# Two token tiles by plain products at the head of pass one, and x's split operands kept in DRAM for pass two

## The chip, the cores and the metric

The kernel runs on one core of a Trainium2 chip. The metric is the device time of one execution in microseconds (us). The engines are PE (TensorE, the matrix unit; PEld is its weight load), DVE (VectorE), ACT (ScalarE), POOL (GpSimd) and SP (SyncE, which issues all DMAs of this kernel).

## The reference

Chunked attention (chunks of 64 tokens) is followed by two feed-forward blocks over 4608 tokens, all in float32:

```python
attn = softmax(0.125 * q_c @ k_c.T) ; x = attn @ v_c     # 8x8 heads of 64, as 4608 x 512
h = x @ w_in          # 512 -> 2048
g = h * np.cos(h)
x2 = g @ w_out        # 2048 -> 512
a = x2 @ w1 ; b = x2 @ w2     # 512 -> 1024 each
out = ((a * b) @ w3) @ w_out2 # 1024 -> 1024 -> 512
```

## The kernel before

**Float32 on PE.** Each operand is split into two parts, a high one rounded for PE and the low rest (`split`: ACT writes the high part, DVE or POOL subtracts to get the low one). A product is then three matmuls (`mm3`: high x high, high x low, low x high; lines 97 to 99).

**Tiles and groups.** The tokens are cut into 9 tiles of 512. The 2048 columns of `w_in` are cut into 8 groups of 256. Pass one takes all nine tiles through groups 0 to 4 and stores its part of x2 (`x2a`); pass two takes them through groups 5 to 7, starting with tile 8 and going on with 0 to 7, and adds (`L529`). Then comes the second block, `ab_mm` and `out_mm`. One round of the loop over `i` is one group of one tile: the products of x with `w_in` (42 matmuls of 256 columns), the chain h*cos(h) on ACT and DVE, and the product of the group before with `w_out` (`x2_mm`, 24 matmuls of 512 columns, in halves `x` and `y`).

**Seven products.** `Seven` computes the 2x2 block product of x and `w_in` with seven block products in place of eight. For this it needs seven operands of x (B11, B21, T2, T1, T3, B22, T4; the T are sums made by `x_sums` and line 408, each of the seven is split by `x_op`) and, of each pair of weight blocks, sums too (lines 175 to 178, split into W pieces 2 and 3). Partial results are combined by DVE out of PSUM into tiles `d` and `e` (lines 440, 450, 452, 459); by this the PSUM bank comes free. `bank_h` has two banks.

**Weights.** A weight arrives as int64 words and is converted by `conv_tick` in a pipeline: load, `conv_a` (ACT line 115, DVE lines 116 and 117), `conv_b` (POOL line 123), `conv_c` (ACT high part, POOL or DVE low part, line 205). Twenty weights (`cq`) are converted in the head and in tile 0. All others are staged through DRAM in pass one and two (`st_load` to `st_lo`, then `pump` loads them, `w<-sd`).

**The order of the work** is written by hand: `START` for the attention of tile 0, and one string of letters per kind of group. In them digits are the steps of `Seven`; `q` is one of five steps of attention for the next tile (scores, exp, scale on POOL, transposes, values); `a A b B` and `c C d D` are the cosine chains of `d` and `e` (`a` ACT, `A` DVE, `b` ACT, `B` DVE); `s` splits g; `w`, `v` are conversions; `l m h r` stage one weight; `S T o` make and split the operands of the next tile's x. In pass one x lies in `xf` and is also stored to `xd` (line 368); in pass two `xf` is loaded from `xd` (line 738) and the seven operands are made again in the last group of each tile (`ORDER3E`).

Of the kernel before, what the change touches and what calls it, by code (L numbers as in the profile page):

```python
# [51 lines left out]
def chunk_attention_two_ffn(  # L52
# [108 lines left out]
    def conv_c(key, lo_eng):  # L161

        pair, second = pair_of(key)
        m = halfway.pop(key).bitcast(F32)
        if not second:
            t = new_w(key if pair is None else (pair, 0))
            nc.scalar.activation(t[:, 0], m, AF.Copy)
            if pair:
                firsts[pair] = m
            return [(lo_eng, t, m)]  # L170
        a = firsts.pop(pair)
        a11, a12, a21, a22 = a[:, 0:256], a[:, 256:512], m[:, 0:256], m[:, 256:512]
        s23 = spare[:, 0]
        s2, s3, s4 = s23[:, 0:256], s23[:, 256:512], spare[:, 1, 0:256]
        nc.vector.tensor_tensor(out=s3, in0=a11, in1=a21, op=ALU.subtract)
        nc.vector.tensor_tensor(out=a21, in0=a21, in1=a22, op=ALU.add)
        nc.vector.tensor_tensor(out=s2, in0=a21, in1=a11, op=ALU.subtract)
        nc.vector.tensor_tensor(out=s4, in0=a12, in1=s2, op=ALU.subtract)
        t, ts = new_w((pair, 1)), new_w((pair, 2))
        t4 = new_s4((pair, 3))  # L180
        for d, x in ((t, m), (ts, s23), (t4, s4)):
            nc.scalar.activation(d[:, 0], x, AF.Copy)
        return [(nc.vector, t, m), (nc.vector, ts, s23), (nc.gpsimd, t4, s4)]
# [4 lines left out]
    def conv_tick(lo_eng=None):  # L188

        last = []  # L190
        if cat[3] < cat[2]:
            key = cq[cat[3]]
            pair, second = pair_of(key)
            if not free(slots, 1 + second) or second and not free(s4s, 1):
                return False
            last = conv_c(key, lo_eng or nc.gpsimd)
            cat[3] += 1
# [155 lines left out]
    def att_values(j, early):  # L353
# [467 lines left out]
```

## Time and profile before

| | us |
|---|---|
| three runs | 1597.18, 1601.99, 1604.14 |
| median | 1601.99 |
| profiled execution, its own time | 1598.41 |
| span of the profile | 1596.6 |
| PE busy | 1503.7 (94%) |
| DVE busy | 1187.9 (74%) |
| ACT busy | 799.2 (50%) |
| POOL busy | 344.8 (22%) |

The profiled execution took 1.8 us more than its span. PE is busy nearly everywhere except at the head and in a stretch of pass two, so a stretch is read by what PE does in it and what it waits for. The boundaries used below are the starts of groups on PE: the first product with `w_in` is at 45.49, tile 1 begins at 145.31, tile 2 at 214.50, tile 3 at 279.10, pass two at 655.9.

### The profile page before, as it was taken

What the parts mean: (1) busy time and instruction counts of PE and PEld (TensorE: products, weight loads), DVE (VectorE), ACT (ScalarE), POOL (GpSimd) and SP (SyncE); (2) the same over time, 40 slices, a digit from 0 to 9 for tenths busy, and PEclk for the clock granted to TensorE, in tenths of its full rate; (3) what the DMA queues carried; (4) which work ended last, traced back from release to release, by engine and by line L of the source; (5) the groups of instructions that cost most, each with busy time, mean ns of one, the idle gap of its engine ahead of it and who ended that gap; (6) DMA issues with size and microseconds to landing.
All of it is one profiled execution on the core that took longest, in us unless ns stands there. A gap on an engine that the chain in (4) does not pass through costs nothing.

```text
span 1596.6 us, 28424 instructions
## 1 busy us (share of the span) xinstructions
PE 1503.7 (94%) x11280; PEld 1358.8 (85%) x11280; DVE 1187.9 (74%) x1868; ACT 799.2 (50%) x1366; POOL 344.8 (22%) x257
## 2 busy tenths in 40 slices
PE   4578999999999999989999999899999999999998
PEld 3467888888888888978888888799999999999997
DVE  7997888887887877788888888736656556566564
ACT  3666887877878776555555555312212212122121
POOL 3766222222322222222222122110000000000000
PEclk8689999999999999999999999999999999999999
DMA  6432445445435435956555454951011011010000
GB/s 207 136 119 73 166 149 175 146 139 167 164 127 166 136 110 201 370 183 220 207 194 196 178 194 171 388 198 53 1 54 53 1 53 54 1 53 30 25 27 27
DMA packets 86100, 212.09 MB, mean 133 GB/s; under 512 B 9552, under 2 KB 12368, under 8 KB 82768
## 3 DMA queue, kind: packets, MB, share of 16 engines
q1 hardware_dynamic: 85968, 210.28, 37.9%
q8 instruction: 89, 1.46, 0.4%
q14 instruction: 43, 0.35, 0.1%
HBM read 133.43 MB, written 76.81 MB: 132 GB/s over the span
## 4 chain that ended last, share of the span: by engine, by line
PE 71%; DVE 14%; DMA 7%; ACT 5%; issue 2%; SPq 1%; DVEq 0%; ACTq 0%
PE acc L97 9%; PE acc L98 9%; PE acc L99 9%; PE ps_hh L97 9%; PE ps_hh L99 8%; PE ps_hh L98 8%; PE ps_aa L97 4%; PE ps_aa L98 4%; PE ps_aa L99 4%; DMA w<-sd 2%; PE ps_at L362 2%; PE ps_s L322 2%; DVE x2a L529 1%; DMA xf<-xd 1%; ACT T L92 1%
## 5 line engine op out<-in xcount | busy, mean ns | idle before, releaser
L500 POOL TENSOR_TENSOR g<-t,g 128x512 fp32r<-128x512 f32 x144 | 203.2, 1432 | 593.0 <-ACT g L499 410.2
L97 PE MATMUL acc<-g,w 128*128 128x512 f32 x576 | 231.1, 401 | 0.0
L92 ACT ACTIVATE phl<-e 128x512 fp32r<-128x512 f32 x72 | 45.5, 632 | 363.6 <-DVE e L598 355.5
L98 PE MATMUL acc<-g,w 128*128 128x512 f32 x576 | 226.9, 394 | 0.1
L99 PE MATMUL acc<-g,w 128*128 128x512 f32 x576 | 226.0, 392 | 0.0
L97 PE MATMUL ps_hh<-T,w 128*128 128x256 f32 x720 | 208.8, 290 | 6.7 <-ACT x L432 6.6
L98 PE MATMUL ps_hh<-T,w 128*128 128x256 f32 x720 | 205.9, 286 | 0.3 <-POOL T L93 0.3
L99 PE MATMUL ps_hh<-T,w 128*128 128x256 f32 x720 | 205.7, 286 | 0.0
L440 DVE TENSOR_TENSOR d<-x,ps_hh 128x512 f32<-128x512 f32 x144 | 98.5, 684 | 136.1 <-PE ps_hh L99 112.7
L97 PE MATMUL ps_hh<-B,w 128*128 128x256 f32 x576 | 167.0, 290 | 1.2 <-ACT B L92 1.2
L98 PE MATMUL ps_hh<-B,w 128*128 128x256 f32 x576 | 163.9, 285 | 3.0 <-DVE B L93 3.0
L99 PE MATMUL ps_hh<-B,w 128*128 128x256 f32 x576 | 163.6, 284 | 0.0
L97 PEld LDWEIGHTS ps_hh<-T,w 128*128 128x128 f32 x720 | 139.9, 194 | 10.1 <-ACT x L432 7.6
L98 PEld LDWEIGHTS ps_hh<-T,w 128*128 128x128 f32 x720 | 139.9, 194 | 1.4 <-POOL T L93 0.7
L99 PEld LDWEIGHTS ps_hh<-T,w 128*128 128x128 f32 x720 | 140.1, 195 | 0.0
L476 ACT ACTIVATE t<-d 128x512 int32<-128x512 f32 x72 | 45.5, 632 | 170.3 <-DVE d L452 168.1
L99 PEld LDWEIGHTS acc<-g,w 128*128 128x128 f32 x576 | 109.3, 190 | 23.9
L98 PEld LDWEIGHTS acc<-g,w 128*128 128x128 f32 x576 | 110.3, 192 | 20.3 <-POOL g L500 0.6
L97 PEld LDWEIGHTS acc<-g,w 128*128 128x128 f32 x576 | 110.3, 191 | 19.8
L98 PE MATMUL ps_aa<-T,w 128*128 128x256 f32 x432 | 122.4, 283 | 0.4 <-DVE T L93 0.4
L97 PE MATMUL ps_aa<-T,w 128*128 128x256 f32 x432 | 122.3, 283 | 0.0
L99 PE MATMUL ps_aa<-T,w 128*128 128x256 f32 x432 | 122.2, 283 | 0.0
(138 smaller groups left out, 3891.3 us busy)
## 6 DMA issues: line engine op xcount, KB each, us to landing
w<-sd SPq DMA_DIRECT2D x63, 512.0 KB, 8.0
sd<-raw SPq DMA_DIRECT2D x104, 256.0 KB, 2.3
qk<-in_q_dram SPq DMA_DIRECT2D x36, 256.0 KB, 3.9
qk<-in_k_dram SPq DMA_DIRECT2D x36, 256.0 KB, 4.1
vt<-in_v_dram SPq DMA_DIRECT2D x36, 256.0 KB, 3.0
x2a<-x2o SPq DMA_DIRECT2D x36, 256.0 KB, 2.6
x2a<-x2a SPq DMA_DIRECT2D x36, 256.0 KB, 7.6
x2d<-x2a SPq DMA_DIRECT2D x36, 256.0 KB, 4.8
```

The source lines that it names most:

```text
L92: nc.scalar.activation(dst[:, 0], src, AF.Copy)
L97: nc.tensor.matmul(ps, a[0], b[0], start=first, stop=False)
L98: nc.tensor.matmul(ps, a[0], b[1], start=False, stop=False)
L99: nc.tensor.matmul(ps, a[1], b[0], start=False, stop=last)
L322: nc.tensor.matmul(s3[r, h], qk[r, 0, h], qk[r, 1, h], start=True, stop=True)
L362: nc.tensor.matmul(o[r, h, t], vt[r, c, h], pt[r, h, t], start=True, stop=True)
L440: nc.vector.tensor_tensor(out=two(self.d), in0=self.x1.unsqueeze(1).to_broadcast([P, 2, 256]), in1=two(p26), op=ALU.add)
L476: nc.scalar.activation(t.bitcast(I32), h, AF.Copy, scale=INV2PI)
L500: nc.gpsimd.tensor_tensor(out=lo, in0=r, in1=f32(hi), op=ALU.subtract)
L529: nc.vector.tensor_tensor(out=t, in0=t, in1=acc[c], op=ALU.add)
```

## The change

**Tiles 0 and 1 by plain products.** For the first ten groups `Plain` replaces `Seven`: eight block products (48 matmuls of 256 columns) straight into two banks, one bank holding what `d` held, the other `e`. No sums of x or of weights are needed, and x has four operands in place of seven. The cosine chain reads the PSUM banks themselves.

**Weights.** In the conversion `conv_b` and every low part move from POOL to DVE; the sums of weight pairs are no longer made there. The converted `w_in` is also stored to DRAM (`wr`), and loaded again in tiles 1 and 2 (`L`), where the sums are made and split (`M`, `H`, `R`), one group per round.

**x in DRAM.** For tiles 2 to 7 the seven split operands are stored in pass one (7 x 512 KB, `xs`) in place of x (1 MB, `xd`). In pass two they are loaded straight into the operands' tiles, each after the last product that reads it (`load_x`), and the last group of such a tile (`ORDER3X`) makes no sums and no splits. Staging takes the eight `wo2` first. All splits of x are on DVE, where `LO` had put some on POOL for the first group strings.

```diff
-ORDER0 = "1sw2qq5qa3cAewbCBxqdyvDqw"
-ORDER1 = "1s2qh5qqa3clAexqbCrmBdyqD"
+ORDER0 = "PsvqQqacvAqCxvqbBdyvDq"
+ORDER0E = "PsvQacvACxobBodyDoo"
+ORDER1P = "PsqMhQqqHaclAxqbCrRmBdyqDL"
+ORDER1PE = "SPsQacATCoobBoxodoDyoo"
+ORDER1 = "1s2qMh5qqHa3clAxqbCrRmBdyqDL"
 ORDER3E = "S1sT25a3cACoobBoxodoDyoo"
+ORDER3X = "1s25a3cACbBxdDy"
...
-        nc.gpsimd.tensor_tensor(out=m, in0=m, in1=raws.pop(key)[:, :, 0].bitcast(I32), op=ALU.add)
+        nc.vector.tensor_tensor(out=m, in0=m, in1=raws.pop(key)[:, :, 0].bitcast(I32), op=ALU.add)
+        if key[0] == "in":
+            nc.sync.dma_start(out=wr[key[1] // 2][:, key[1] % 2], in_=m.bitcast(F32))
...
+    def sum_load(g):
+        pair = ("in", g)
+        sp["at"] = pair, new_w((pair, 2))
+        nc.sync.dma_start(out=f32(W[pair, 2]), in_=wr[g])
+
+    def sum_make():
...
+        nc.vector.tensor_tensor(out=s3, in0=a11, in1=a21, op=ALU.subtract)
+        nc.vector.tensor_tensor(out=s1, in0=a21, in1=a22, op=ALU.add)
+        nc.vector.tensor_tensor(out=s2, in0=s1, in1=a11, op=ALU.subtract)
+        nc.vector.tensor_tensor(out=s4, in0=a12, in1=s2, op=ALU.subtract)
...
+    def sum_lo():
+        for d, x in sp.pop("parts"):
+            nc.vector.tensor_tensor(out=d[:, 1], in0=x, in1=f32(d[:, 0]), op=ALU.subtract)
...
+    def x_op(op, keep=None):
 
         d = X[op].rearrange("p s (c t) -> p s c t", c=2)
-        split(d, xv[op], nc.vector if los[-1][OPS.index(op)] == "v" else nc.gpsimd)
+        split(d, xv[op], nc.vector)
+        if keep in xs:
+            nc.sync.dma_start(out=xs[keep][op], in_=f32(X[op]))
...
+    class Plain:
...
+        def half(self, blocks):
+            p = bank_h()
+            for n, (e, ops) in enumerate(blocks):
+                w, ps = self.w[e], p[:, 256 * n:256 * n + 256]
+                for c in range(4):
+                    m, x, t = slice(P * c, P * c + P), X[ops[c // 2]], slice(256 * (c % 2), 256 * (c % 2) + 256)
+                    mm3(ps, (w[:, 0, m], w[:, 1, m]), (x[:, 0, t], x[:, 1, t]), c == 0, c == 3)
+            return p
+
+        def stepP(self):
+            self.d = self.half([(0, ("B11", "B21")), (1, ("T1", "B22"))])
+
+        def stepQ(self):
+            self.e = self.half([(0, ("T1", "B22")), (1, ("B11", "B21"))])
...
-            return ORDER3E if end else ORDER3B if nth else ORDER3
+            return (ORDER3X if k_tile in xs else ORDER3E) if end else ORDER3B if nth else ORDER3
...
+            def load_x(op):
+                nc.sync.dma_start(out=f32(X[op]), in_=xs[k_tile][op])
+
+            z = Plain(("in", g)) if i < 2 * GA else Seven(
+                ("in", g), (bank_h,) * 4, False, load_x if ps and end and k_tile in xs else None)
...
-                if nth == 0:
+                if nth == 0 and k_tile not in xs:
                     nc.sync.dma_start(out=xf, in_=xd[k_tile] if k_tile + 1 < NTILE else x2d[order[0]])
```

DVE in the second group of tile 0 before: the cosine chain (L481, L491) with conversions and the sums of a weight pair (L175 to L178) between its steps.

```order
L481 SCALAR_TENSOR_TENSOR t<-d,t 128x512
L116 TENSOR_SCALAR cw<-raw 128x512
L117 SCALAR_TENSOR_TENSOR cw<-raw,cw 128x512
L481 SCALAR_TENSOR_TENSOR t<-e,t 128x512
L491 TENSOR_TENSOR t<-t,d 128x512
L175 TENSOR_TENSOR spare<-cw 128x256
L176 TENSOR_TENSOR cw<-cw 128x256
L177 TENSOR_TENSOR spare<-cw 128x256
L178 TENSOR_TENSOR spare<-cw,spare 128x256
```

The same place in the changed kernel: the chain is L529 and L539 there and reads the bank `ps_hh`, the conversion is L128, L121, L122, L195.

```order
L529 SCALAR_TENSOR_TENSOR t<-ps_hh,t 128x512
L358 TENSOR_REDUCE sm<-ex 128x8
L359 TENSOR_SCALAR sm<-sm 128x8
L361 RECIPROCAL rc<-sm 128x8
L529 SCALAR_TENSOR_TENSOR t<-ps_hh,t 128x512
L128 ISA cw<-raw,cw 128x1024
L121 TENSOR_SCALAR cw<-raw 128x512
L122 SCALAR_TENSOR_TENSOR cw<-raw,cw 128x512
L195 TENSOR_TENSOR w<-cw,w 128x512
L539 TENSOR_TENSOR t<-t,ps_hh 128x512
```

The weight sums are gone from here, and a conversion (one POOL instruction of it now on DVE, as L128) stands between the chain's two halves.

DVE in pass two before, from the last group of a tile into the first of the next: the splits of x (L93) and one sum (L408) stand among the chain's steps and ahead of L440, which frees a bank.

```order
L481 SCALAR_TENSOR_TENSOR t<-e,t 128x512
L93 TENSOR_TENSOR B_119<-xf,B_119 128x512
L93 TENSOR_TENSOR B_120<-xf,B_120 128x512
L491 TENSOR_TENSOR t<-t,d 128x512
L93 TENSOR_TENSOR T_121<-spare,T_121 128x512
L408 TENSOR_TENSOR xf<-xf,spare 128x2x256
L93 TENSOR_TENSOR T_122<-spare,T_122 128x512
L93 TENSOR_TENSOR T_123<-xf,T_123 128x512
L491 TENSOR_TENSOR t<-t,e 128x512
L93 TENSOR_TENSOR B_124<-xf,B_124 128x512
L93 TENSOR_TENSOR T_125<-xf,T_125 128x512
L440 TENSOR_TENSOR d<-x_9088,ps_hh 128x512
```

The same place in the changed kernel (L529 and L539 are the chain, L466 is what L440 was):

```order
L529 SCALAR_TENSOR_TENSOR t<-e,t 128x512
L539 TENSOR_TENSOR t<-t,d 128x512
L539 TENSOR_TENSOR t<-t,e 128x512
L466 TENSOR_TENSOR d<-x_9112,ps_hh 128x512
L291 TENSOR_TENSOR raw<-cw,raw 128x512
```

Eight instructions ahead of L440 are gone (three sums more stood earlier in the group).

SP at that place in the changed kernel: the seven loads (L733) stand between the loads of x2 (L588) and the first store of the next staged weight (L294).

```order
L588 DMA x2a<-x2a_133 128x512 x4
L733 DMA B_166<-xs3B_96 128x1024
L733 DMA B_167<-xs3B_97 128x1024
L733 DMA T_168<-xs3T_98 128x1024
L733 DMA T_169<-xs3T_99 128x1024
L733 DMA T_170<-xs3T_100 128x1024
L733 DMA B_171<-xs3B_101 128x1024
L733 DMA T_172<-xs3T_102 128x1024
L294 DMA sd_9144<-raw 128x512
```

Before, L540 (the loads of x2) is followed there by the store L273 at once; the load of `xf` stood one group earlier.

## Rows read from the trace of the kernel before

**Rows 1.** Windows: us; PE, PEld, DVE, ACT, POOL busy; PEclk; DMA share; GB/s.

```profile
0.00:45.49 45.49, 19.43 (x272) 16.88 (x273) 35.12 (x57) 19.59 (x35) 17.73 (x19) 0.83 0.59 199
45.49:145.31 99.82, 71.18 (x578) 61.81 (x579) 89.78 (x106) 60.47 (x100) 69.66 (x48) 0.80 0.37 124
145.31:214.50 69.19, 66.15 (x603) 58.65 (x602) 58.07 (x94) 52.65 (x85) 23.02 (x18) 0.98 0.40 134
214.50:279.10 64.60, 64.60 (x604) 57.14 (x602) 55.63 (x96) 52.26 (x85) 17.83 (x14) 1.00 0.48 160
764.70:1005.60 240.90, 227.42 (x1333) 201.96 (x1332) 207.08 (x325) 136.91 (x247) 53.79 (x36) 0.99 0.55 190
```

**Rows 2.** Timeline of the head: start, duration, engine, line, operation, idle time before.

```profile
26.65 0.42 DVE L116 TENSOR_SCALAR cw<-raw 128x512 uint32<-128x512 uint32 x1
27.10 0.69 DVE L117 SCALAR_TENSOR_TENSOR cw<-raw,cw 128x512 uint32<-128x512 uint32 x1
27.71 0.69 DVE L205 TENSOR_TENSOR w<-cw,w 128x512 fp32r<-128x512 f32 x1
27.93 1.60 POOL L123 TENSOR_TENSOR cw<-cw,raw 128x512 int32<-128x512 int32 x1 [3.07 <-ACT raw L115]
28.43 1.39 DVE L116 TENSOR_SCALAR cw<-raw 128x512 uint32<-128x512 uint32 x1
...
29.85 1.65 DVE L117 SCALAR_TENSOR_TENSOR cw<-raw,cw 128x512 uint32<-128x512 uint32 x1
```

**Rows 3.** Groups by line and form: busy us, mean ns of one; idle before.

```profile
L242 DVE CUSTOM_DVE_ANT_0 cw<-raw,cw 128x1024 uint16<-128x1024 uint16 x52 | 36.0, 693 | 7.0 <-DVE cw L240 0.5
...
L326 DVE TENSOR_TENSOR ex<-ps_s,mx 128x512 f32<-128x512 f32 x36 | 24.9, 692 | 2.7
...
L337 DVE TENSOR_REDUCE sm<-ex 128x8 f32<-128x512 f32 x36 | 24.4, 678 | 0.9 <-ACT ex L332 0.9
```

**Rows 4.** The same view: POOL's part of g's split, and its scale.

```profile
L500 POOL TENSOR_TENSOR g<-t,g 128x512 fp32r<-128x512 f32 x144 | 203.2, 1432 | 593.0 <-ACT g L499 410.2 <-DVE B L93 143.6 <-PE ps_hh L99 39.2
...
L341 POOL TENSOR_TENSOR ex<-ex,rc 128x512 f32<-128x512 f32 x32 | 33.5, 1045 | 72.2 <-DVE rc L340 72.2
```

**Rows 5.** Timeline of DVE in tile 0's fourth group, where no conversion is left.

```profile
132.60 0.69 DVE L491 TENSOR_TENSOR t<-t,d 128x512 f32<-128x512 f32 x1 [2.13 <-ACT t L487]
...
134.35 0.69 DVE L491 TENSOR_TENSOR t<-t,e 128x512 f32<-128x512 f32 x1 [1.06 <-ACT t L487]
```

**Rows 6.** Timeline of PE: matmuls of 256 columns, first at half clock, then full.

```profile
70.89 0.41 PE L97 MATMUL ps_hh<-B,w 128*128 128x256 f32 x1
71.11 0.41 PE L98 MATMUL ps_hh<-B,w 128*128 128x256 f32 x1
...
71.47 0.28 PE L97 MATMUL ps_hh<-T,w 128*128 128x256 f32 x1
71.59 0.28 PE L98 MATMUL ps_hh<-T,w 128*128 128x256 f32 x1
```

**Rows 7.** Windows over three groups of pass two; columns as in Rows 1.

```profile
764.70:775.20 10.50, 10.50 (x67) 9.54 (x66) 7.45 (x13) 6.49 (x12) 2.55 (x2) 1.00 0.48 187
775.20:788.50 13.30, 13.30 (x80) 11.83 (x79) 12.40 (x20) 6.32 (x13) 3.15 (x2) 1.00 0.35 120
788.50:806.40 17.90, 15.00 (x80) 13.12 (x79) 15.83 (x28) 10.99 (x20) 2.50 (x2) 0.90 0.87 286
```

**Rows 8.** Timeline across these groups: DVE's late L440, and the stop of PE.

```profile
778.98 0.68 DVE L440 TENSOR_TENSOR d<-x,ps_hh 128x512 f32<-128x512 f32 x1
...
780.70 1.51 DVE L239 TENSOR_SCALAR cw<-raw 128x512 uint32<-128x512 uint32 x1
...
797.85 0.39 PE L97 MATMUL ps_hh<-B,s 128*128 128x256 f32 x1 [2.90 <-DVE d L440]
```

**Rows 9.** DMA at its densest, 1000 to 1060 us: moved; KB each, us to landing.

```profile
DMA packets 7528, 22.65 MB, mean 378 GB/s; under 512 B 843, under 2 KB 843, under 8 KB 7268
...
w<-sd SPq DMA_DIRECT2D x22, 512.0 KB, 9.0
```

More of the change, by code (lines that the diff above doesn't have):

```diff
@@ L159, in pair_of, with conv_c, conv_tick @@
         return None, 0
-    def conv_c(key, lo_eng):
+    def conv_c(key):
         pair, second = pair_of(key)
         m = halfway.pop(key).bitcast(F32)
[L165 to L183, printed above, removed]
+        t = new_w((pair, second) if pair else key)
+        nc.scalar.activation(t[:, 0], m, AF.Copy)
+        return t, m
     held = [False, False]
     cq, cat = [], [0, 0, 0, 0]
-    def conv_tick(lo_eng=None):
-        last = []
+    def conv_tick():
+        last = None
         if cat[3] < cat[2]:
-            key = cq[cat[3]]
-            pair, second = pair_of(key)
-            if not free(slots, 1 + second) or second and not free(s4s, 1):
+            if not free(slots, 1):
                 return False
-            last = conv_c(key, lo_eng or nc.gpsimd)
+            last = conv_c(cq[cat[3]])
             cat[3] += 1
@@ L203, in conv_tick @@
             cat[1] += 1
-        for eng, t, w in last:
-            eng.tensor_tensor(out=t[:, 1], in0=w, in1=f32(t[:, 0]), op=ALU.subtract)
+        if last:
+            t, w = last
+            nc.vector.tensor_tensor(out=t[:, 1], in0=w, in1=f32(t[:, 0]), op=ALU.subtract)
         while cat[0] < min(len(cq), cat[1] + 2):
@@ L209, in conv_tick, with sum_hi @@
         return True
+    sp = {}
+    def sum_load(g):
[3 more added lines that the diff above has]
+    def sum_make():
+        assert not held[0] and not held[1]
+        held[1] = True
+        pair, w = sp["at"]
+        a, m = f32(w[:, 0]), f32(w[:, 1])
+        a11, a12, a21, a22 = a[:, 0:256], a[:, 256:512], m[:, 0:256], m[:, 256:512]
+        s2, s3, s4, s1 = spare[:, 0, 0:256], spare[:, 0, 256:512], spare[:, 1, 0:256], spare[:, 1, 256:512]
+        nc.vector.tensor_tensor(out=s3, in0=a11, in1=a21, op=ALU.subtract)
+        nc.vector.tensor_tensor(out=s1, in0=a21, in1=a22, op=ALU.add)
+        nc.vector.tensor_tensor(out=s2, in0=s1, in1=a11, op=ALU.subtract)
+        nc.vector.tensor_tensor(out=s4, in0=a12, in1=s2, op=ALU.subtract)
+        sp["parts"] = [(W[pair, 1][:, :, 0:256], s1), (w, spare[:, 0]), (new_s4((pair, 3)), s4)]
+    def sum_hi():
+        for d, x in sp["parts"]:
+            nc.scalar.activation(d[:, 0], x, AF.Copy)
+    def sum_lo():
+        for d, x in sp.pop("parts"):
+            nc.vector.tensor_tensor(out=d[:, 1], in0=x, in1=f32(d[:, 0]), op=ALU.subtract)
+        sp.pop("at")
+        held[1] = False
     def need(*keys):
@@ L366, in att_values @@
         nc.scalar.activation(xf[:, :, P * jj:P * jj + P], o, AF.Copy)
-        if jj == TT // P - 1 and n < NTILE - 1:
+        if jj == TT // P - 1 and n < NTILE - 1 and n not in xs:
             nc.sync.dma_start(out=xd[n], in_=xf)
@@ L459, in step3, with __init__ @@
             nc.vector.tensor_tensor(out=self.e, in0=self.e, in1=p, op=ALU.add)
+    class Plain:
+        def __init__(self, pair):
+            self.w = [W[pair, i] for i in range(2)]
+            self.done = ["B11", "B21", "T1", "B22"]
+        def half(self, blocks):
[10 more added lines that the diff above has]
+            self.e = self.half([(0, ("T1", "B22")), (1, ("B11", "B21"))])
     def bank_h():
@@ L658, in chunk_attention_two_ffn @@
             if i == GA:
+                sq.extend(("wo2", j) for j in range(FB2))
                 for g in range(GA, G1):
@@ L729, in chunk_attention_two_ffn @@
                 elif op == "o":
-                    x_op(z.done[n_o])
+                    if i < GA and not n_o:
+                        x_plain()
+                    x_op((z.done if i < GA or i >= 2 * GA else OPS)[n_o], n + 1 if ps == 0 else None)
                     n_o += 1
```

54 lines of the change are left out of this document (29 added, 25 removed).

## The prediction

> **What bounds the kernel now.** I read the windows by stage first, for the share of PE in each, then the timeline where that share is below one, then the groups by form for durations. The first product of pass one starts at 45.49. Tile 0 then takes 99.82 us, of which PE is busy 71.18 at a mean clock of 0.80 of full, and DVE 89.78: DVE sets the pace there [rows 1]. Tile 1 takes 69.19, tile 2 64.60 with PE busy all the time: from there on pass one is as fast as its products. In pass two PE is not: over the six tiles from 764.70 to 1005.60 it is busy 227.42 of 240.90 [rows 1]. A tile without stops is there 10.50 + 2 x 13.25 = 37.0 us (a group of 10.50, two that also hold weight folding of about 2.7); the third group shown took 17.90 [rows 7], because PE stood 2.90 us for L440, and the clock behind that stop was lower (0.90 over that group) [rows 7, 8]. So the six tiles could be 240.9 - 6 x 37.0 = 18.9 us shorter. The rest (second block) is untouched.
>
> **The head.** Up to the last split of tile 0's x the changed DVE order holds five first parts of a conversion (0.42 + 0.69), four of what POOL did (0.69), three low parts (0.69) [rows 2, 3], four chunks of attention (0.69 twice, 0.68, two short ones, scale 0.69: about 3.1 each) and four splits of x (0.69): 5.6 + 2.8 + 2.1 + 12.4 + 2.8 = 25.7 us. Before, DVE was busy 35.12 of 45.49, idle 10.4 [rows 1]; with the same idle time the first product starts at 36.1. The last splits now wait for the last chunk of attention with nothing left to do beside it; I add 2 us and take 38 (bounds 36 and 45.5).
>
> **Tile 0.** Per group with attention DVE has four conversions of 0.42 + 0.69 + 0.69 + 0.69 = 2.49, attention 2.4, and four steps of the cosine chain at 0.69: 15.2 us. To this come two things. POOL still runs g's split (2 x 1.43) and the scale (1.05) [rows 4], and a DVE instruction of two operands in SBUF that meets POOL takes 1.39 in place of 0.42, or 1.65 in place of 0.69 [rows 2], some 1.0 more: 3.0 for three. (Without POOL's conversions this is what is left of a cost that was much larger: POOL was busy 69.66 us in this tile [rows 1], it will be about 4 per group, 20.) And DVE may wait for the cosine, which in a group without conversions cost 2.13 + 1.06 [rows 5]; with four conversions to do I take 0.8, bounds 0 and 3.2. Sum 19.0 per group, four times; the fifth has no attention and two half conversions, 48 x 0.12 + 24 x 0.23 = 11.2 of PE (256 columns start every 0.12 at the higher clock level, every 0.21 or 0.22 at the lower [rows 6]; 0.23 is what a group of 10.50 without attention [rows 7] leaves to its 24 wide ones) and 1.2 for the first splits: 12.4. Tile 1 then starts at 38 + 76 + 12.4 = 126.4.
>
> The Trainium skill, page "SBUF — State Buffer", section "SBUF: two separate sides", says that DVE and GpSimd hold their shared port pair for a whole instruction while the other stands. By that rule the three meetings cost up to all of POOL's 3.9 us, 20 per group, and the total would be 4 us more. The pairs in [rows 2] show about 1.0 per meeting, less than POOL's 1.60, and I go by these.
>
> **Tile 1.** PE has 6 matmuls more in each of five groups: 30 x 0.12 = 3.6 on top of 64.6. Three of its groups also make weight sums: four DVE instructions, about 0.43 each, and three splits, 3.2 us, in front of the second half of the cosine chain, which alone frees the bank that the next group's first product needs. In [rows 1] DVE has 9 us of 64.6 to spare in such a tile, and the combining of seven products is gone here (about 2.5 per group), so most of it fits: I take 1.0 for each of the three (bounds 0 and 3.2), 71.3 in all. Tile 2 starts at 197.7 in place of 214.50: 16.8 us earlier. The two sums left over fall in tile 2, beside seven products; staging already has such groups with PE never idle, so nothing for them.
>
> The seven stores per tile in pass one add 2.6 MB to 64.6 us, 41 GB/s on 160, with 0.48 of the DMA time used [rows 1]: hidden. They stand on SP's queue ahead of the next load of q and k, which has a whole group of slack.
>
> **Pass two.** Six transitions lose three sums, one more sum and seven splits: DVE 7.6 us of 34.5 per tile, ACT 4. Two stops go with them: in the last group, where L440 waited behind the sums, and in the second group of the next tile. There L440 started at 778.98, behind the last splits, though its products had ended 1.4 us earlier; DVE then runs without a break to the late L440 of the next group, with POOL slowing one of them to 1.51 [rows 8]. Starting 1.4 earlier, and with g's split earlier too (another 1.4), the longest stop of this kind shrinks from 2.9 to nearly nothing; the short ones go. I take 17 of the 18.9. The price is 7 x 512 KB to load in place of 1 MB. At the densest the DMAs moved 378 GB/s on average, and a load of 512 KB then landed after 9.0 us [rows 9]; 3.7 MB are 9.7 us of that, 1 MB of x2 ahead of them 2.8. The first operand is free 0.8 us after the group starts and needed at 10.5, the last is needed some 17 us after the start: they land at about 5 to 14, each some 3 to 5 us in time. So no wait, bounds 0 and 8 us per transition (if all seven came last).
>
> **Sum.** Span 1596.6 - 16.8 - 17.0 = 1562.8, and 1.8 for what lies around it: 1565. The execution that I argue from took 1598.4, the median of the three runs is 1602.0.
>
> **Rivals.** *DVE alone paces tile 0* (0.10): no wait for the cosine, and POOL meets DVE only once; 16.2 per group and no loss in tile 1. For it: four of the chain's steps read PSUM and may not meet POOL at all. 14 us less: 1551.
>
> *The loads come late* (0.11): SP issues in order and one queue carries all; staging stores, the folded weights and x2 stand before the seven loads. If each transition waits 2.8 us, pass two gains nothing: 1582. Against it: only 0.55 of the DMA time is used there [rows 1], 0.75 with the loads. The Trainium skill, page "DMA: Bandwidth & Descriptors", section "Queues, rings and completion order", says each DMA engine takes its descriptors in the order of the ring; by that the loads wait for all that was issued earlier, which is how the 14 us above are worked out.
>
> *Tile 0 stays as slow as it was* (0.10): the chain from the scale through transposes and cosine to the next bank sets it, not DVE's sum. Only pass two pays: 1581.
>
> *The banks make it slower* (0.08): `Plain` holds both banks until the whole cosine chain has read them, so PE cannot run ahead. If PE stands long enough in each group, the clock falls to the lower level as in [rows 6], and 48 products take 48 x 0.213 = 10.2, and 24 wide ones and attention (3.0 per group, what 64.60 leaves beside five groups of 10.50) nearly twice their time, some 10 and 5.5: 25.7 us per group. Tile 2 would start at 38 + 8 x 25.7 + 2 x 20.5 = 285, 70 us later than before: 1652. It turns the gain of pass two into a loss from a mean of 19.4 us per group over the ten (16.0 forecast). For it: PE's clock of 0.80 in tile 0 [rows 1]. Against it: in tile 1 nothing but three groups' sums stands in the way.
>
> **How the numbers follow.** The forecast has 0.61, with its own range of 1551 to 1577 (16 to 21 us per group of tile 0, 13 to 18.9 in pass two). To hold eight in ten I go from 1548 to 1586, which takes in the DVE rival, the late loads and the slow tile 0, and leaves out the banks. A measurement can tell about 0.5% (8 us) from no change. Faster by more: 0.88, all but the banks and a part of the late loads; within: 0.06; slower: 0.06, the banks.
>
> **What would show it.** Right: first product near 38; tile 0 near 88 us with DVE busy over 90%; tile 1 near 71 with stops of about 1 us before the first product of a group, behind L539; tiles of pass two at 37 to 38 us without waits of PE for L466. Wrong: PE waiting for a DMA into B or T at the start of a tile; a clock of 0.8 or less in tile 1; groups of tile 0 over 21 us.

## The result and the profile after

The changed kernel takes 1572.98 us (median of four runs, 1572.75 to 1574.5) against 1600.33 for the kernel before (four runs, 1597.18 to 1604.14): a ratio of 0.9827, 95% interval 0.9808 to 0.9847, 27 us less. The forecast was 1565 with a range of 1548 to 1586. The profiled execution took 1572.75, with a span of 1571.0, 25.6 less than before.

The windows by stage of the changed kernel, with the columns of [rows 1]. The last one is six tiles of pass two counted from the start of a tile, a group later than the window of [rows 1]; the kernel before takes 240.90 counted in either way.

```profile
0.00:37.90 37.90, 17.94 (x272) 15.37 (x272) 22.96 (x44) 13.36 (x22) 0.70 (x6) 0.88 0.63 208
37.90:126.80 88.90, 73.17 (x610) 64.14 (x609) 69.03 (x108) 59.12 (x96) 16.63 (x12) 0.86 0.55 181
126.80:200.20 73.40, 70.20 (x633) 61.79 (x632) 46.70 (x87) 51.10 (x84) 17.33 (x14) 0.98 0.40 136
200.20:273.20 73.00, 66.80 (x603) 58.26 (x602) 57.95 (x103) 53.68 (x88) 17.76 (x14) 0.98 0.50 167
768.20:991.50 223.30, 222.16 (x1334) 198.78 (x1333) 164.00 (x265) 117.22 (x208) 48.51 (x36) 1.00 0.79 280
```

| stage | before | after | difference | forecast |
|---|---|---|---|---|
| to the first product | 45.5 | 37.9 | -7.6 | -7.5 |
| tile 0 | 99.8 | 88.9 | -10.9 | -11.4 |
| tile 1 | 69.2 | 73.4 | +4.2 | +2.1 |
| tile 2 | 64.6 | 73.0 | +8.4 | 0 |
| tiles 3 to 8 | 376.8 | 376.8 | 0 | 0 |
| first tiles of pass two | 119.3 | 118.2 | -1.1 | 0 |
| six tiles of pass two | 240.9 | 223.3 | -17.6 | -17 |
| the rest | 580.5 | 579.5 | -1.0 | 0 |

So the shortfall against the forecast has one address: the groups of tiles 1 and 2 in which weight sums are made. The timeline of the changed kernel around the first of them, all engines (start, duration, engine, line, operation, idle time before and what ended it):

```profile
143.06 0.89 SPq L573 DMA_DIRECT2D x2a<-x2o  x2
144.05 0.51 SPq L332 DMA_DIRECT2D vt<-in_v_dram  x1
144.61 0.64 SPq L207 DMA_DIRECT2D w<-wr  x1
...
149.84 0.43 DVE L216 TENSOR_TENSOR spare<-w 128x256 f32<-128x256 f32 x1 [2.93 <-DMA w<-wr]
...
151.44 0.68 DVE L358 TENSOR_REDUCE sm<-ex 128x8 f32<-128x512 f32 x1
...
152.71 1.04 POOL L362 TENSOR_TENSOR ex<-ex,rc 128x512 f32<-128x512 f32 x1 [6.42 <-DVE rc L361]
...
153.80 0.65 PE L369 MATMUL ps_at<-ident,ex 128*128 128x128 f32 x4 [2.61 <-POOL ex L362]
```

It reads from the bottom up. PE stands before the transposes (L369) until POOL has scaled the softmax (L362); POOL stands until DVE has the reciprocal; DVE's row sum (L358) is queued behind the weight sums, and the first of these (L216) stands 2.93 us for the pair loaded from `wr`. That load was issued at 144.61 only, behind the stores of `x2o` and the load of `vt`: SP, which issues in the order of the program, had stood 21.8 us at the first of these stores until ACT had copied `x2o` (L572). The four sums themselves take 0.43 each and start about 0.45 apart. The waits of DVE over tiles 1 and 2 (us in total, times, longest):

```profile
DVE mx L345 <- PE ps_s L343: 14.4, 7, 4.4
DVE t L539 <- ACT t L535: 7.6, 9, 3.1
DVE spare L216 <- DMA w<-wr: 6.8, 2, 3.9
```

L216 waits twice, 6.8 us in all: the two groups that are long. Tile 1's second group took 18.65 where its neighbours take 14.34 and 14.54, tile 2's second group 19.90 where an undisturbed one takes 13.5.

In tile 0 the forecast's number came out, and its reason did not. DVE is busy 69.03 of 88.90, 78% and not over 90%. PE's waits there (us in total, times, longest):

```profile
PE ps_at L369 <- POOL ex L362: 13.7, 4, 4.8
PE ps_hh L102 <- DVE t L539: 1.3, 1, 1.3
PE ps_at L383 <- ACT pt L371: 0.7, 1, 0.7
```

Four stops of 2.7 to 4.8 us, one in each group with attention, all of them for the scale. DVE itself stood, in the same stretch, for ACT:

```profile
DVE t L539 <- ACT t L535: 9.3, 6, 2.2
DVE w L195 <- ACT w L173: 5.2, 6, 2.0
DVE t L529 <- ACT t L524: 2.9, 2, 2.2
```

An engine that waits 17.4 us for others is hardly what sets the pace by its sum of work; the experiment that moves the scale, below, puts this to the test. In pass two the loads of x's operands hold nobody up: there is no wait of PE for them, five of the six tiles take 37.0 us, and the DMA view of that stretch (KB each, median us from issue to landing) shows where they land:

```profile
DMA packets 25316, 62.75 MB, mean 280 GB/s; under 512 B 2809, under 2 KB 4345, under 8 KB 25170
...
T<-xs3T SPq DMA_DIRECT2D x4, 512.0 KB, 7.7
T<-xs4T SPq DMA_DIRECT2D x4, 512.0 KB, 6.4
...
B<-xs3B SPq DMA_DIRECT2D x3, 512.0 KB, 6.2
B<-xs4B SPq DMA_DIRECT2D x3, 512.0 KB, 4.8
```

### The profile page after: what moved, and what is told of

It reads as the page before. It is cut to its first block, busy times and chain, and to the rows that moved or that the text cites. A ratio compares the mean times of both kernels' runs of the same rounds, so it can differ in the third digit from the quotient of the medians.

```text
span 1571.0 us, 28515 instructions
## 1 busy us (share of the span) xinstructions
PE 1505.1 (96%) x11340; PEld 1360.7 (87%) x11340; DVE 1105.3 (70%) x1804; ACT 771.9 (49%) x1313; POOL 263.6 (17%) x206
## 4 chain that ended last, share of the span: by engine, by line
PE 82%; DVE 7%; DMA 5%; ACT 3%; issue 1%; SPq 1%; POOL 0%; DVEq 0%; ACTq 0%; POOLq 0%
PE acc L102 11%; PE acc L103 11%; PE ps_hh L102 11%; PE acc L104 10%; PE ps_hh L104 10%; PE ps_hh L103 10%; PE ps_aa L103 5%; PE ps_aa L102 5%; PE ps_aa L104 5%; PE ps_s L343 2%; PE ps_at L383 2%; DMA w<-sd 1%; PE ps_at L369 1%; DMA xf<-xd 1%; DMA w<-wr 1%
## 5 line engine op out<-in xcount | busy, mean ns | idle before, releaser
L548 POOL TENSOR_TENSOR g<-t,g 128x512 fp32r<-128x512 f32 x144 | 198.4, 1399 | 610.8 <-ACT g L547 514.0
L97 ACT ACTIVATE phl<-e 128x512 fp32r<-128x512 f32 x72 | 45.5, 632 | 364.8 <-DVE e L646 356.7
L466 DVE TENSOR_TENSOR d<-x,ps_hh 128x512 f32<-128x512 f32 x134 | 91.8, 685 | 159.1 <-PE ps_hh L104 107.5
L102 PE MATMUL ps_hh<-T,w 128*128 128x256 f32 x680 | 196.5, 289 | 0.3 <-ACT x L458 0.3
L103 PE MATMUL ps_hh<-T,w 128*128 128x256 f32 x680 | 193.2, 284 | 0.0
L104 PE MATMUL ps_hh<-T,w 128*128 128x256 f32 x680 | 193.1, 284 | 0.0
L102 PE MATMUL ps_hh<-B,w 128*128 128x256 f32 x656 | 189.4, 289 | 2.9 <-DVE t L539 1.8
L103 PE MATMUL ps_hh<-B,w 128*128 128x256 f32 x656 | 186.1, 284 | 0.0
L104 PE MATMUL ps_hh<-B,w 128*128 128x256 f32 x656 | 186.0, 284 | 0.0
L102 PEld LDWEIGHTS ps_hh<-B,w 128*128 128x128 f32 x656 | 125.9, 192 | 10.1 <-DVE t L539 2.5
L102 PEld LDWEIGHTS ps_hh<-T,w 128*128 128x128 f32 x680 | 131.1, 193 | 3.3 <-ACT x L458 0.6
L103 PEld LDWEIGHTS ps_hh<-T,w 128*128 128x128 f32 x680 | 131.2, 193 | 0.6
L104 PEld LDWEIGHTS ps_hh<-T,w 128*128 128x128 f32 x680 | 131.2, 193 | 0.0
L103 PEld LDWEIGHTS ps_hh<-B,w 128*128 128x128 f32 x656 | 126.0, 192 | 4.4
L102 PEld LDWEIGHTS acc<-g,w 128*128 128x128 f32 x576 | 111.1, 193 | 20.3
L104 PEld LDWEIGHTS ps_hh<-B,w 128*128 128x128 f32 x656 | 125.9, 192 | 0.0
L103 PE MATMUL ps_aa<-T,w 128*128 128x256 f32 x432 | 122.4, 283 | 0.4 <-DVE T L98 0.4
```

What stands on the lines that cost most here:

```text
L97: nc.scalar.activation(dst[:, 0], src, AF.Copy)
L102: nc.tensor.matmul(ps, a[0], b[0], start=first, stop=False)
L103: nc.tensor.matmul(ps, a[0], b[1], start=False, stop=False)
L104: nc.tensor.matmul(ps, a[1], b[0], start=False, stop=last)
L466: nc.vector.tensor_tensor(out=two(self.d), in0=self.x1.unsqueeze(1).to_broadcast([P, 2, 256]), in1=two(p26), op=ALU.add)
L548: nc.gpsimd.tensor_tensor(out=lo, in0=r, in1=f32(hi), op=ALU.subtract)
```

## The experiments

Spans and windows are those of the profiled executions; ratios are against the kernel before on the same chip (its median was 1598.6 to 1601.4 in the groups of runs).

**The late load of the pairs of weights.** `L` moves ahead of the step for which SP waits.

```diff
-ORDER1P = "PsqMhQqqHaclAxqbCrRmBdyqDL"
+ORDER1P = "PsqMhQqqHaclAxqbCrRLmBdyqD"
-ORDER1 = "1s2qMh5qqHa3clAxqbCrRmBdyqDL"
+ORDER1 = "1s2qMh5qqHa3clAxqbCrRLmBdyqD"
```

> The changed kernel with one letter moved: the load of a stored pair of weights (L) stands right behind the low parts of the sums before it (R), ahead of the attention chunk whose load of v makes SP wait, and no longer at the end of the group. Theory (the sums are cheap, their load is late: issued at 144.61 and 219.34, it lands 2.9 and 3.9 us after DVE stands before L216, and PE stops 3.0 and 5.0 us): both stops go, tile 1 takes about 70, tile 2 about 66 to 68 in place of 73.0, the whole about 1565 (7 to 9 us less than 1573). Rival (DVE is too full in those groups, so the sums themselves cost what tile 2 lost): L216 no longer waits, but tile 2 still takes 71 or more and the whole stays within 3 us of 1573.

Measured: 1564.63 us, ratio 0.978 (0.9763 to 0.9797). Tiles 1 and 2 of this kernel:

```profile
126.40:195.60 69.20, 68.40 (x633) 60.84 (x632) 46.55 (x87) 50.98 (x84) 17.33 (x14) 1.00 0.40 137
195.60:263.60 68.00, 65.20 (x603) 57.13 (x602) 58.42 (x103) 53.46 (x88) 17.77 (x14) 1.00 0.53 180
```

SP issues the first of these loads at 119.98 in place of 144.61. L216 no longer waits, the two long groups take 14.53 and 14.92, and 9.6 us of span are gone (8.4 of the median time): the theory holds. What the sums themselves cost can now be read: in tile 1, 0.2 per group (14.53 against 14.34); in tile 2 at most 3.4, in its first two groups (15.48 and 14.92 for 13.5).

**x's operands alone,** on the kernel before.

```diff
+ORDER3X = "1s25a3cACbBxdDy"
-            return ORDER3E if end else ORDER3B if nth else ORDER3
+            return (ORDER3X if k_tile in xs else ORDER3E) if end else ORDER3B if nth else ORDER3
```

(with `xs`, its stores, `load_x` and the condition on the load of `xf`, as in the change)

> The kernel before, with x's split operands kept in DRAM and the shorter order at the end of pass two's tiles, and nothing else of the change. Theory (the two parts add up, and this one is worth what the six tiles showed): pass one as before within 1 us up to the third tile, the six tiles of pass two about 223, the whole 17 to 18 us below before, about 1583. Rival (pass two gets faster only since POOL no longer converts or makes low parts for staging there): the six tiles stay above 232 and the whole is less than 9 us below before.

Measured: 1579.0 us, ratio 0.9877 (0.9857 to 0.9896), 20 us less than before. The six tiles:

```profile
779.20:1002.50 223.30, 222.16 (x1333) 198.79 (x1333) 163.90 (x265) 117.23 (x208) 48.58 (x36) 1.00 0.78 278
```

223.30 again, with POOL's part in the conversions as it was: the rival falls. The whole gained 2 to 3 us more than expected, which its interval (17 to 23 us) does not tell from 17.6.

**The head alone:** the change with

```diff
-    xs = {n: {op: dram.tile([P, 2, TT], F32, name=f"xs{n}{op}")
-              for op in ("B11", "B21", "T2", "T1", "T3", "B22", "T4")} for n in range(2, NTILE - 1)}
+    xs = {}
```

> The changed kernel without x's operands in DRAM: the head with plain products and the sums made later are alone. Theory: first product at 38, tile 2 starts at 200, tile 3 at 273, pass two's six tiles 240 to 241 as before, the whole 6 to 8 us below before (about 1593). Rival (the seven stores per tile in pass one cost something, being on SP's queue ahead of the load of wr and of the chunks): tile 1 and tile 2 are 3 us or more shorter than in the changed kernel and the whole is 10 us or more below before.

Measured: 1591.92 us, ratio 0.9948 (0.993 to 0.9966), 7.4 less than before; first product 38.3, tile 2 at 198.6, tile 3 at 271.1, the six tiles 241.0. The parts add up by medians: 20.3 and 7.4, 27.7, where the change gave 27.4. By the spans of the profiled executions they are 15.5 and 7.3 for 25.6; the one of x's operands alone was the slowest of its four, and loses some 5 us in the first tiles of pass two. The stores in pass one cost 2 us at most.

**The scale earlier in tile 0.** Only one `q` moves, so that the row sum and the scale stand ahead of one conversion and of `A`; no work is added or removed. (The expectation has the conversion move behind `A` too; in the string it stays ahead of `A`.)

```diff
-ORDER0 = "PsvqQqacvAqCxvqbBdyvDq"
+ORDER0 = "PsvqQqqacvACxvqbBdyvDq"
```

> The changed kernel with one conversion of each of tile 0's groups moved from before the second chain of t (A) and the softmax's scale to behind them. Theory (tile 0 is set by the chain from the softmax through the scale, the transposes and the cosine to the bank, and the conversions that stand on DVE ahead of them delay it): each of four groups is about 2.5 to 3 us shorter, tile 0 takes 77 to 80 in place of 88.9, the whole is about 10 us below 1573. Rival, as the prediction had it (DVE's sum of work sets the group, so that the order within it does not matter): tile 0 stays within 2 us of 88.9.

Measured: 1565.33 us, ratio 0.9785 (0.9768 to 0.9802). Tile 0 and PE's waits in it:

```profile
38.30:118.80 80.50, 68.27 (x611) 60.25 (x609) 70.59 (x108) 59.58 (x96) 16.99 (x12) 0.94 0.60 200
```

```profile
PE ps_at L369 <- POOL ex L362: 6.0, 4, 2.0
PE ps_hh L102 <- DVE t L539: 5.3, 3, 2.9
```

Tile 0 became 8.4 us shorter while DVE's busy time rose by 1.6. It is just above the expected 77 to 80, and far from the rival's 88.9: DVE's sum did not set the tile; the order did. Two things changed: the wait for the scale fell from 13.7 to 6.0 (4.0 came back as waits for the bank, 5.3 for 1.3), and with shorter stops PE's granted clock (PEclk in the windows) was 0.94 of full on average in place of 0.86, and the same products took PE 68.27 in place of 73.17.

**All of this in one kernel,** and a third order at tile 1's end.

```diff
-ORDER1PE = "SPsQacATCoobBoxodoDyoo"
+ORDER1PE = "SPsQacATCobBodDoxooyoo"
```

> The changed kernel with three orders mended: the load of a stored pair of weights early (as in the first experiment), the softmax's scale early in tile 0 (as in the fourth), and at the end of tile 1 the last cosine step of the group moved ahead of three of the seven splits of x, since the next group's second product waits 1.3 us for the bank that it frees. Theory (the three losses lie one behind the other, so the gains add up): 9.6 + 8.5 + 1 us off the changed kernel's span of 1571.0, about 1552, and some 1554 measured. Rival (one bound lies under both: DVE, fuller now, takes back what an earlier start gives): 1559 or more.

Measured: 1557.89 us, ratio 0.9736 (0.9722 to 0.975), span 1557.3. The span missed the expected 1552 by 5, and the time lies nearer the rival's number. Tile 0 took 81.0, tiles 1 and 2 69.2 and 68.2, so 7.9 and 9.0 of the two gains came; the third edit gave nothing (68.0 without it), and the first tiles of pass two took 120.6 in place of 118.2 (118 to 121 in all the other runs but one). The rival's reason is not borne out where it was looked for: the first two gains lie side by side. This is faster than both kernels.

**Scores first as well, and the scale on DVE.** Both have the early load and the early scale, without the third order.

```diff
-ORDER0 = "PsvqQqqacvACxvqbBdyvDq"
+ORDER0 = "PsqvQqqacvACxvqbBdyvDq"
```

> The changed kernel with the early load of the pairs of weights and the early scale, and in tile 0 the attention scores as well moved ahead of the group's first conversion; tile 1's end is as in the change. Theory (the chain from the scores through softmax, scale, transposes and cosine to the bank sets tile 0, and one more conversion of 2.5 us stands ahead of it on DVE): each of four groups is 1 to 2.5 us shorter than the 17.1 to 17.7 of the kernel with three orders, tile 0 takes 71 to 77 in place of 81.0, the whole 1548 to 1554. Rival (past this point DVE's sum of work, about 71 of tile 0's 81, is the bound): tile 0 stays above 79, the whole 1556 to 1558.

```diff
-        (nc.vector if early else nc.gpsimd).tensor_tensor(
+        (nc.vector if early or j < 8 else nc.gpsimd).tensor_tensor(
```

> The changed kernel with the early load of the pairs of weights and the early scale, and in tile 0 the scale itself on DVE (0.69) in place of POOL (1.05 and the meetings with DVE). Theory (the chain sets tile 0, and this takes a hand-over and some 0.4 to 1 us out of it): each of four groups is 0.5 to 1.5 us shorter than 17.1 to 17.7, tile 0 takes 75 to 79, the whole 1551 to 1556. Rival (DVE's sum of work is the bound by now and this adds to it): tile 0 takes 81 or more, the whole is 1557 or more.

Measured: 1555.07 us (ratio 0.9734, 0.972 to 0.9748) and 1556.18 us (0.9738, 0.9725 to 0.975); tile 0 takes 79.7 in both, against 80.5 with the early scale alone. Both theories asked for more: scores first gained 1.3 on the kernel with three orders where 4 was the least expected, and has the rival's tile; the scale on DVE lies between its two expectations. The rival's reason doesn't hold either, since with the scores first DVE is busy 64.06 of 79.70. The gain that the theory asked for did come in two of four groups: with the scores first the third and fourth take 16.24 each, 1.4 less than with the three orders, while the first and second take 0.6 and 1.1 more (17.2 and 18.7, at a granted clock of 0.80 and 0.85). What sets the last ten us of tile 0 is left open. These two and the kernel with three orders can't be told apart by their intervals.

**Conversions on DVE alone,** on the kernel before.

```diff
-LO = "vvvpppp"
+LO = "vvvvvvv"
-        nc.gpsimd.tensor_tensor(out=m, in0=m, in1=raws.pop(key)[:, :, 0].bitcast(I32), op=ALU.add)
+        nc.vector.tensor_tensor(out=m, in0=m, in1=raws.pop(key)[:, :, 0].bitcast(I32), op=ALU.add)
-        return [(nc.vector, t, m), (nc.vector, ts, s23), (nc.gpsimd, t4, s4)]
+        return [(nc.vector, t, m), (nc.vector, ts, s23), (nc.vector, t4, s4)]
-            last = conv_c(key, lo_eng or nc.gpsimd)
+            last = conv_c(key, nc.vector)
```

> The kernel before with one thing taken from the change: everything that POOL converted (the sums of the bit patterns, the low parts of weights and of x) is done by DVE, with the seven products and their weight sums as they were. Theory, as in the prediction (meeting POOL makes DVE's instructions 1.0 us longer, and POOL's conversions are most of those meetings): DVE's work in tile 0 rises by some 14 to 20 instructions of 0.69 but falls in what each takes, its busy time stays near 90 or falls to about 80, and tile 0 takes 88 to 95 in place of 99.8; the whole 1588 to 1595. Rival (tile 0 and the head got faster because of the plain products, that is without weight sums, sums of x and combining of products, and moving work to DVE by itself costs time): tile 0 takes 100 or more, the whole is 1599 or more.

Measured: 1594.3 us, ratio 0.9963 (0.9951 to 0.9975). Tile 0 and tile 1:

```profile
45.20:142.30 97.10, 69.94 (x578) 61.65 (x579) 85.60 (x136) 60.17 (x100) 25.57 (x18) 0.83 0.38 128
142.30:209.00 66.70, 64.70 (x604) 57.23 (x603) 56.61 (x98) 52.86 (x85) 17.40 (x14) 1.00 0.41 139
```

DVE does 30 instructions more in tile 0 and is busy 4.2 us less (0.63 us for one in place of 0.85 in [rows 1]): the cost of meeting POOL is real. But the tile gains 2.7 only, short of the expected 88 to 95, tile 1 another 2.5, and the whole about 6, which is in the expected range. By subtraction, the rest of tile 0's 10.9 and nearly all of the head's 7.6 (the first product is at 45.2 here) belong to the plain products and what they do without; no run has the plain products with POOL's conversions, so how the two act on each other is not shown.

**Which engine's relief shortens pass two.** Idle work is put where x's sums and splits stood in the last group of six tiles, on `xf`, which is free there: on DVE (ten of the eleven instructions; the one sum that stood among the splits is left out), on ACT, on both as they were chained; and at last with the load of `xf` that three of DVE's instructions then wait for. The last kernel leaves out the loads of x's operands in these tiles, so that its output is not the reference's; only its time is used.

```diff
-ORDER3X = "1s25a3cACbBxdDy"
+ORDER3X = "ZZ1sZ25a3cACZZbBZxZdZDyZZ"
+                elif op == "Z":
+                    nc.vector.tensor_tensor(out=xf[:, 0], in0=xf[:, 1], in1=xf[:, 2], op=ALU.subtract)
```

> The changed kernel with ten idle subtractions of 128x512 on DVE in the last group of each of six tiles of pass two, where the three sums and the seven low parts of x stood before; the values made are not used, ACT is not given anything to do. Theory (it was DVE's queue that made PE stop, L440 behind the sums and splits): each is 0.69 or less, and the six tiles go from 223.3 back to 235 to 241. Rival (the wait was for ACT's seven copies, or for the chain between the two): the six tiles stay below 228.

```diff
+ORDER3X = "1s25a3cACZZbBZxZdZDyZZ"
+                elif op == "Z":
+                    nc.scalar.activation(xf[:, 0], xf[:, 1], AF.Copy)
```

> The changed kernel with seven idle copies of 128x512 on ACT in the last group of each of six tiles of pass two, where the high parts of x stood before; the values made are not used, DVE is not given anything to do. Theory (DVE's queue is what counted): the six tiles stay at 223 to 226. Rival (ACT's copies, 0.63 each, delayed the cosine and so the bank): 232 or more.

```diff
+ORDER3X = "ZZ1sZ25a3cACYYbBYxYdYDyYY"
+                elif op == "Y":
+                    n_o += 1
+                    hi = xf[:, 2 * (n_o % 2) + 1]
+                    nc.scalar.activation(hi, xf[:, 2], AF.Copy)
+                    nc.vector.tensor_tensor(out=xf[:, 0], in0=xf[:, 2], in1=hi, op=ALU.subtract)
```

> The changed kernel with the idle work of both engines put back in the last group of each of six tiles of pass two: three subtractions on DVE, and seven times a copy of 128x512 on ACT with a subtraction on DVE that waits for it, where x's sums and splits stood; only the load of xf and the stores are still away, and x's operands still come from DRAM. Theory (the two engines' work adds up through the waits of one for the other: DVE's alone cost 3.0 us, ACT's alone 11.5): the six tiles go to 238 to 241, all of the 17.6 us. Rival (about 3 us of the gain are of another kind, the waits of DVE for the load of xf, 4.4 us in these tiles before): 232 to 237.

```diff
-                ("in", g), (bank_h,) * 4, False, load_x if ps and end and k_tile in xs else None)
+                ("in", g), (bank_h,) * 4, False, None)
-                if nth == 0 and k_tile not in xs:
-                    nc.sync.dma_start(out=xf, in_=xd[k_tile] if k_tile + 1 < NTILE else x2d[order[0]])
+                if nth == 0:
+                    nc.sync.dma_start(out=xf, in_=xd[min(k_tile, 1)] if k_tile + 1 < NTILE else x2d[order[0]])
```

> The kernel with both engines refilled, and with the load of xf put back at the place where it stood before (1 MB per tile, of other values, and the three idle subtractions stand behind it); the seven loads of x's operands in those six tiles are left out, so that the DMAs move what they moved before (x keeps the operands of an earlier tile). Theory (6.9 of the 17.6 us are stops of PE in the last group of a tile, behind DVE's first sum, which waits for xf: 4.4 us in four of these tiles before): DVE waits for xf again, last groups of 11.5 to 15 come back, the six tiles take 238 to 242. Rival (what is missing are the waits of the splits for operands that are still in use, which idle work does not have): the six tiles stay at 233 to 236, with all last groups at 10.50.

| in the six tiles | whole, us | ratio (interval) | six tiles, us |
|---|---|---|---|
| the change | 1572.98 | 0.9827 (0.9808 to 0.9847) | 223.3 |
| DVE refilled | 1578.14 | 0.9862 (0.9844 to 0.988) | 226.3 |
| ACT refilled | 1584.14 | 0.9902 (0.9882 to 0.9921) | 234.8 |
| both refilled | 1585.44 | 0.9917 (0.9903 to 0.9931) | 234.0 |
| both, and the load of `xf` | 1594.44 | 0.9964 (0.9945 to 0.9983) | 245.3 |
| before | | | 240.9 |

The theory that went in, DVE's queue, fell: DVE's ten instructions cost 3.0 us over six tiles, ACT's seven copies 11.5, each in the range of the rival. The first of the six tiles has 2.2 and 4.6 of these; in the other five DVE's cost 0.2 per tile and ACT's 1.4. The timeline of the first group of a tile with DVE refilled, whose group starts at 846.40:

```profile
847.60 1.14 ACT L547 ACTIVATE g<-t 128x512 fp32r<-128x512 f32 x2
848.35 2.99 POOL L548 TENSOR_TENSOR g<-t,g 128x512 fp32r<-128x512 f32 x2 [7.95 <-ACT g L547]
...
850.12 0.67 DVE L466 TENSOR_TENSOR d<-x,ps_hh 128x512 f32<-128x512 f32 x1
850.72 1.18 DVE L291 TENSOR_TENSOR raw<-cw,raw 128x512 fp32r<-128x512 f32 x1
851.81 0.41 DVE L260 TENSOR_SCALAR cw<-raw 128x512 uint32<-128x512 uint32 x1
```

and with ACT refilled, whose group starts at 853.31:

```profile
856.40 1.14 ACT L547 ACTIVATE g<-t 128x512 fp32r<-128x512 f32 x2
857.15 2.99 POOL L548 TENSOR_TENSOR g<-t,g 128x512 fp32r<-128x512 f32 x2 [9.86 <-ACT g L547]
...
856.53 0.69 DVE L466 TENSOR_TENSOR d<-x,ps_hh 128x512 f32<-128x512 f32 x1 [1.43 <-ACT x L458]
...
858.09 0.90 DVE L291 TENSOR_TENSOR raw<-cw,raw 128x512 fp32r<-128x512 f32 x1 [0.87 <-ACT raw L285]
858.92 1.52 DVE L260 TENSOR_SCALAR cw<-raw 128x512 uint32<-128x512 uint32 x1
...
873.46 0.68 DVE L466 TENSOR_TENSOR d<-x,ps_hh 128x512 f32<-128x512 f32 x1
```

g's split (L547) starts 1.2 us after the group in the one and 3.1 after it in the other, behind the copies; so do ACT's copies for staging (L285), for which DVE stands 0.87; and POOL's half of the split then runs into staging's first instruction on DVE (1.52 for 0.41). L260 ends 5.8 us after the start of the group in the one and 7.1 in the other, 7.0 in the kernel before (780.70 + 1.51 in [rows 8], the group starting at 775.20). DVE doesn't make up for it: the next group's L466 comes at 873.46, and that group takes 14.65 in place of 13.24. The same holds in every kernel. In the third of the six tiles (us from the start of the first or the second group; L260 and L466 are L239 and L440 in the kernel before):

| | the change | DVE refilled | ACT refilled | both | before |
|---|---|---|---|---|---|
| L260 ends, first group | 5.2 | 5.8 | 7.1 | 7.2 | 7.0 |
| L466 starts, second group | 5.0 | 5.6 | 6.9 | 7.0 | 6.8 |
| the second group takes | 13.24 | 13.33 | 14.65 | 14.69 | 14.51 |

L466 follows L260 by the same 13.0 us each time. With DVE refilled it is 0.6 late, of which PE feels 0.1; with ACT refilled it is 1.9 late, and the group is 1.4 longer.

Both engines refilled give no more than ACT alone, where 238 to 241 was expected, and every last group stays at 10.50. In the kernel before four of these took 11.7 to 14.9: of the 17.6 us by which it is slower over the six tiles, its second groups have 9.5 and its last groups 8.2. The waits of DVE over the same stretch, in the kernel before:

```profile
DVE spare L392 <- DMA xf<-xd: 4.4, 4, 1.5
```

and of DVE and of PE in the kernel with the load put back:

```profile
DVE xf L751 <- DMA xf<-xd: 5.1, 4, 1.4
...
PE ps_hh L102 <- DVE d L466: 16.8, 10, 3.1
```

With the load four of the last groups take 11.9 to 14.7 and PE stops ten times for L466 (before, ten times for the same step, L440 there: 13.5 us). The wait costs more than its own length, because it pushes the sums that stand behind it into POOL's half of g's split. In the last group that starts at 884.29, before, POOL is at that split from 886.24 to 889.56:

```profile
886.05 0.69 DVE L392 TENSOR_TENSOR spare<-xf 128x512 f32<-128x512 f32 x1 [1.48 <-DMA xf<-xd]
886.77 1.67 DVE L393 TENSOR_TENSOR spare<-xf,spare 128x512 f32<-128x512 f32 x1
888.36 1.75 DVE L396 TENSOR_TENSOR xf<-xf 128x512 f32<-128x512 f32 x1
```

Without the load, with both engines refilled, all three sums take 0.69. So the gain has two sources of like size: ACT's copies, and a sum at the head of DVE's queue that waited for a load. The last kernel comes out 4.4 above the stretch it imitates, and outside its expected 238 to 242, so the split between the two by these runs is good to a few us. One reason can be seen: two sums are slowed in three of its four late groups, against one of the four before.

## Why the prediction was right, and where it was not

*The head.* 37.9 for 38, by two errors that cancel. DVE is busy 22.96 there, not 25.7: two of the four splits run only after the first product, and instructions that follow at once overlap a little. It is idle 14.9, not 12.4, most of it before the scores, whose products wait for the load of k:

```profile
PE ps_s L343 <- DMA qk<-in_k_dram: 9.0, 3, 4.5
DVE mx L345 <- PE ps_s L343: 10.3, 3, 5.3
```

The forecast took its idle time from the kernel before and added 2 us, without asking when k lands; that the sum came out was luck.

*Tile 0.* 88.9 for 88.4, by the wrong step. The forecast summed DVE's work per group (15.2 + 3.0) and added 0.8 of waiting. The second to fourth group show DVE busy 16.6 to 17.4, and idle 2.6 to 3.5:

```profile
55.63:76.00 20.37, 17.71 (x141) 15.54 (x141) 17.35 (x27) 14.08 (x23) 4.01 (x3) 0.82 0.53 169
76.00:95.44 19.44, 16.03 (x144) 13.73 (x140) 16.85 (x27) 13.74 (x23) 4.30 (x3) 0.91 0.57 177
95.44:115.50 20.06, 17.18 (x145) 14.54 (x141) 16.58 (x26) 12.87 (x21) 4.28 (x3) 0.83 0.37 118
```

The first group took 17.7 and the fifth 11.3, where 19.0 and 12.4 were forecast. The chain from the scale through the transposes and the cosine, which the forecast gave to a rival, is what held the tile up: moving one `q` gave 8.4 us. That rival's price was wrong in turn: it had the tile stay at 99.8. That a number agrees isn't evidence for the sum behind it; the busy share, which the forecast had named as its test, was.

The meetings of DVE and POOL were put at 3.0 per group. Three kinds of DVE's instructions in tile 0 have a longer mean than the undisturbed 0.69, 0.69 and 0.42 (busy us, mean ns of one, idle before):

```profile
L128 DVE CUSTOM_DVE_ANT_0 cw<-raw,cw 128x1024 uint16<-128x1024 uint16 x16 | 14.4, 898 | 0.0
L122 DVE SCALAR_TENSOR_TENSOR cw<-raw,cw 128x512 uint32<-128x512 uint32 x15 | 12.3, 821 | 0.5
...
L121 DVE TENSOR_SCALAR cw<-raw 128x512 uint32<-128x512 uint32 x15 | 9.6, 637 | 0.0
```

16 x 0.21 + 15 x 0.13 + 15 x 0.22 = 8.6 us, 2.1 per group. (L121 reads one operand and is slowed as well, so "two operands in SBUF" was too narrow.) With ACT refilled L260 comes at 858.92 and ends 0.3 after POOL's pair of instructions (857.15 to 860.14): it stood until POOL was done. The Trainium skill, page "SBUF — State Buffer", section "SBUF: two separate sides", has it so: who comes first holds the port pair for a whole instruction. Here the trace agrees; this meeting cost 1.1 us, less than one of POOL's instructions (1.5), as DVE came in the middle of it.

*Tile 1 and tile 2.* This is the step that failed (its sum is also off by 0.1: 64.6 + 3.6 + 3 x 1.0 is 71.2): "The two sums left over fall in tile 2, beside seven products; ... so nothing for them", and 1.0 for each sum in tile 1. In tile 1 the sums cost less than was allowed (0.2 each), and the stops behind L539 that were named as a sign came to 0.4 in the two tiles together; in tile 2 the sums cost at most 3.4 with all that goes with them, once their load is early; the load itself was not counted. The prediction asked of each new DMA whether there was bandwidth, and not what stands ahead of it on SP's queue in the group where its result is wanted. Moving it gave 9.6 us of span and 8.4 of the median time, as much as the 8 by which the time missed.

*Pass two.* 17.6 for 17. The recoverable 18.9 and the two places of the stops were read rightly. The reason was half right. Of the two things named for the second group, L440 starting earlier and g's split earlier, the second is what counts: L466 comes later after the group's start with DVE refilled (3.7) than with ACT refilled (3.2), and PE stops with the latter. What was read rightly is that DVE then runs without a break to the late step of the next group. For the last group the sums were named, but not that the first of them waited for `xf`, nor that POOL slowed those behind it.

*The rivals.* PE's waits for the banks came to 1.3 us in tile 0 and 0.4 in tiles 1 and 2, far from 70. The loads were not late. DVE alone as the pace of tile 0 is refuted with the forecast's own step.

## What to carry to other kernels

A load that is added to an in-order queue is priced by what stands ahead of it there and by when its result is wanted, before bandwidth is asked; here one letter in an order string was worth 9.6 us. When work is taken off two engines at once, refill them one at a time with idle work: the one with the larger sum need not be the one that paid. And if a forecast of the kind "this engine's sum sets the pace" comes out, look at that engine's waits before believing it.

## What the runs showed that was not expected

Ten more instructions of DVE (0.69 each, 6.9 us) cost a tile of 37 us 0.5 on average and 0.2 in five of six, seven of ACT (0.62 each, 4.3 us) 1.9 and 1.4, though ACT was busy 117 of 223 us and DVE 164: slack at the right moment counts, and the busier engine had more of it. A wait of DVE of 0.9 to 1.5 us for a load made four groups 1.2 to 4.4 us longer, as it pushed DVE's next instructions into POOL's. In tile 0 more than half of what an earlier scale gave (4.9 of 8.4 us) came through PE's own clock, 0.94 of full for 0.86, once the stops of up to 4.8 us were down to 2.9 and less.
